# A fused retention and SwiGLU kernel: the first segment in another order, weight words and side tables in fewer transfers

## The chip, the cores and the metric

The kernel runs on one core of a Trainium2 chip. The metric is the device time of one execution in microseconds (us). A core has five engines that run side by side, each through its own list of instructions in order: TensorE (PE; loads of its stationary operand are shown as PEld), VectorE (DVE), ScalarE (ACT), GpSimd (POOL) and SyncE (SP), which here issues nearly all transfers (DMA). Matrix products land in PSUM, here eight banks of 128 x 512 floats; everything else lies in SBUF.

## The reference

Retention with a decay per head, then a gated feed-forward block, in 32-bit floats:

```python
B, H, S, D = 4, 8, 768, 64            # q, k, v
gamma = 1.0 - 2.0 ** (-5.0 - np.arange(H))
for t in range(S):
    state = gamma * state + einsum('bhd,bhe->bhde', k[:, :, t], v[:, :, t])
    y[:, :, t] = einsum('bhd,bhde->bhe', q[:, :, t], state) / sqrt(D)
x = y.transpose(0, 2, 1, 3).reshape(3072, 512)
g = x @ w_gate                        # 512 x 1536
out = (g * sigmoid(g) * (x @ w_val)) @ w_out   # 1536 x 512
```

The weights come in as 64-bit floats and are read as pairs of 32-bit words.

## The kernel before

**Tiling.** Retention is computed in chunks of 128 positions. For a chunk, the scores `k q` are masked with a decay table; y is the old state times the scaled q plus own values times the masked scores; the state is carried on with a scaled k. The 3072 tokens are cut into four segments of 768 (3 chunks of each of two sequences). Each segment goes through three stages: retention makes xT; the up stage walks over 12 units of 128 of the 1536 features; the down stage adds up 6 x 12 products in six banks. Each 2 x 2 block product of the up stage is done with seven products instead of four (Strassen's scheme in Winograd's form), of sums of x and of differences of weights. In segments 1 to 3 operands are split in three parts for a faster product form (L826, L876); in segment 0 products are in plain 32-bit floats (L665). The retention of the next segment runs as side steps within a down stage (L903 to L960).

**Segment 0.** Six chunks are loaded (`cs`, in order: pairs of first, second and third positions of two sequences). While its up stage runs, the weights are brought in: 24 pieces, 0 to 11 up (128 features of w_gate and w_val, 1 MB of words) and 12 to 23 down (w_out, 0.5 MB). A piece is loaded (L170), converted from two words to one float in five steps, turned into differences (L251) or split (L236), and stored to DRAM for the later segments. The conversion: `a` on ACT rescales the high word (L209), `b` on ACT makes the sign bits in a PSUM bank (L213), `S` on DVE joins them (L223), `c` on ACT scales the low word (L217), `C` on POOL adds it (L232). The raw words lie in the buffers `rawp` and `loads`; a load waits on SP until the piece before it in its buffer is through with `C`.

**The order is written out by hand** in strings of tokens. A token is a letter, a number and perhaps a part: `l4:1` loads q (0 is k transposed, 1 q transposed, 2 v, 3 k) of chunk 4; `A` loads a piece of the decay tables; `s` scores, `m` values and the copy of y to xT (L483), `x` sums of x (L635), `t` state, `g` decay of a state, `k`/`q` scaling on POOL, `K`/`Q` on DVE, `w` warm-up products; `U` loads a weight piece into a buffer, `a b S c C` convert it, `T` makes differences, `F` splits, `Z` stores; `L` loads a side table (L498), `P` loads inputs of segment 1; `M` multiplies gate and value of a unit (L679). `START` (L291) runs before the up stage. `beside` (L297) is a list of 73 slots parted by `|`, six for each of the 12 units: `up` (L655) runs a slot after each of its parts through `aside` (L389). Since every engine keeps its order, a token's place fixes its place in the list of each engine that it uses.

**A unit of the up stage** (L683 to L703), in PE's order: B11 times x11 into bank x, copied to `p1` by ACT (L684); the gates product of the unit before, which waits for that unit's DVE add L698, since it goes on in the bank that L698 reads; T1 times s1 into wb, copied to `p5` (L689); T2 times s2 into x, copied to `u2` (L692); B22 times s4 into wb, which goes on after the copy L689, and the add L695; T3 times s3 into x, and the add L698; B21 times x12 into z, and the add L701. A product is four matmul records of 384 columns here.

**Side steps.** Two chunks are worked at once, one of each sequence. `scale_k2` (L599) scales k of a chunk by eight activations on ACT, one a head. `load_side` (L498) brings in the masks of one group of heads for one half of the partitions: a full part, and a shifted part that keeps the second 64 positions. Planned times in `WHEN` (L325) order the side steps. `finish` (L880) takes a finished bank to SBUF, on DVE for odd tiles and on ACT for even ones, and stores it.

Of the kernel before, what the change touches and what calls it, by code (L numbers as in the profile page):

```python
# [17 lines left out]
P = 128  # L18
# [7 lines left out]
L = 3  # L26
# [23 lines left out]
def tile_retnet_swiglu(  # L50
# [101 lines left out]
    T3, B22, B12, T1, B11, B21, T2, T4 = 0, 1, 2, 2, 3, 4, 5, 6  # L152
# [17 lines left out]
    def load_piece(piece, where=0):  # L170
        kind, a = piece
        wide = w_gate.dtype != F32
        if kind == "up":
            new_wt(a)
            gate, val = (w[:, ts(a, P)].rearrange("(c p) f -> p c f", p=P)
                         for w in (w_gate, w_val))
            parts = [(val[:, ds(KH, KH)], 0), (val[:, ds(0, KH)], 1), (gate, 2)]
        else:
            parts = [(w_out[ts(a, P)], 0)]
# [4 lines left out]
        for src, i in parts:  # L184
            if wide:
                src = src.bitcast(U32)
            t = to[:, i:].rearrange("p a b -> p (a b)")
            if kind == "up":
                c = src.shape[1]
                t = t[:, : c * src.shape[2]].rearrange("p (c f) -> p c f", c=c)  # L190
            nc.sync.dma_start(out=t, in_=src)  # L191

    signs = {}
    stores = {}

    def words_of(piece):
        w, slot, n = span(piece)
        d = w[:, ds(slot, n)].rearrange("p a b -> p (a b)")
        r = raw[piece].rearrange("p a (n two) -> p (a n) two", two=2)
        return d, r[:, :, 0], r[:, :, 1]  # L200


    def convert_a(piece, own, part=None):


        if piece in raw:
            d, lo, hi = words_of(piece)
            if part in (0, None):
                act(d, hi.bitcast(F32), AF.Copy, scale=2.0 ** -112)  # L209
            if part in (1, None):  # L210
                signs[piece] = []
                for i, o in enumerate(own):
                    act(banks[o].bitcast(I32), d[:, ts(i, 512)], AF.Prelu, scale=2.0 ** 94,  # L213
                        alpha=2.0 ** 127)
                    signs[piece].append(banks[o])
            if part in (2, None):
                act(lo.bitcast(I32), lo, AF.Copy, scale=2.0 ** -29)  # L217

    def convert_b(piece):
        if piece in raw:  # L220
            u = words_of(piece)[0].bitcast(U32)
            for i, t in enumerate(signs.pop(piece)):
                stt(u[:, ts(i, 512)], u[:, ts(i, 512)], 3, t.bitcast(U32),  # L223
                    op0=ALU.logical_shift_left, op1=ALU.bitwise_or)


    def convert_c(piece, halves=1):
        if piece in raw:
            d, lo, hi = words_of(piece)
            n = d.shape[1] // halves  # L230
            for i in reversed(range(halves)):
                pool(d[:, ts(i, n)].bitcast(I32), d[:, ts(i, n)].bitcast(I32),  # L232
                     lo[:, ts(i, n)].bitcast(I32), op=add)
            del raw[piece]
# [16 lines left out]
    def sums_t(piece, parts=range(3)):  # L251
# [5 lines left out]
        for o, x, y in [((pair, w[:, ds(B22, 2)], w[:, ds(B12, 2)])),  # L257
# [3 lines left out]
        if parts[-1] == 2:  # L261
# [5 lines left out]
    sign_banks = {0: (0, 1), 1: (4, 5)}  # L267

    parts = {
        "s": lambda n: scores(cs[n]), "m": lambda n: mix(cs[n]), "x": lambda n, *p: sums_x(n, *p),  # L270
        "g": lambda n: decay(cs[n]), "t": lambda n: state(cs[n]), "w": lambda n: warm_up(n),
        "k": lambda n: scale_k(cs[n]), "q": lambda n: scale_q(cs[n]),
        "K": lambda n: scale_k(cs[n], nc.vector), "Q": lambda n: scale_q(cs[n], nc.vector),
        "S": lambda n: convert_b(pieces[n]),
        "C": lambda n: convert_c(pieces[n], 1 + (n == 0)), "T": lambda n, *p: sums_t(pieces[n], *p),
        "U": lambda n, p: load_piece(pieces[n], p[0]), "l": lambda n, p: load_chunk(n, p[0]),
# [3 lines left out]
        "L": lambda n: load_side(n // 2, n % 2),  # L280
        **{p: lambda n, i=i: convert_a(pieces[n], sign_banks.get(n, (6, 7)), i)
           for i, p in enumerate("abc")}}

    def do(order):
        for o in order.split():
# [6 lines left out]
        l0:0 l1:0 A0 A1 l0:2 l1:2 A2 l0:3 l2:0 l2:1 l1:3 l2:2 l2:3 l3:0 l3:1 l3:2 l3:3 l4:0  # L292
        l4:1 U0:0 l4:2 l5:0 l5:1 l5:2 U1:2 l4:3 l5:3 s0 w6 s1 m0 m1 K0 t0 K1 s2 t1 g2 g3 Q2
        s3 m2 x0:0 x0:1 x0:2 x0:3 k2 q3 t2 s4 a0 b0 m3 k3 t3 q4 c0 s5 S0 x1:0 x1:1 x1:2 x1:3
        m4 a1 q5 C0 U2:0 m5 x2:0 T0:0 x2:1 T0:1 x2:2 x2:3 T0:2 U3:4 U12:6
    """
    beside = """  # L297
        b1 | c1 S1 U13:7 | g5 g4 C1 | a2 T1:0 U14:8 | U15:9 | c2 b2 T1:1 a3 |
        S2 T1:2 | b3 C2 Z0 S3 | Z1 T2:0 | c12 c3 a12 C3 M0 b12 | U5:0 a13 T2:1 | T2:2 |
        S12 C12 T3:0 M1 |  | T3:1 F12:0 U4:2 Z2 | T3:2 a4 b4 U6:4 S4 a5 Z3 | F12:1 c4 F12:2  # L300
            C4 | b5 S5 T4:0 |
        T4:1 c6 L0 | M2 U16:6 c5 C5 | b13 c13 S13 | L1 C13 U7:2 a6 a14 | F12:3 T5:0 U8:0 b6
            | T4:2 T5:1 S6 F13:0 |
        F13:1 Z4 F13:2 b14 | F13:3 Z13 C6 M3 S14 | a15 a7 b7 c7 | T5:2 T6:0 T6:1 Z12 | S7
            T6:2 Z5 L3 c14 b15 | C14 U18:8 F14:0 |
        S15 C7 F14:1 | M4 F14:2 F14:3 | a8 U9:4 U17:7 Z6 c15 | C15 a16 Z14 | L2 F15:0 T7:0 |
            F15:1 c8 b8 |
        T7:1 S8 | U10:2 F15:2 a9 M5 C8 F15:3 | a17 T7:2 c16 b16 | U19:9 T8:0 b9 | U11:0 S16
            P0 C16 S9 F16:0 | P1 b17 |
        F16:1 T8:1 F16:2 Z15 c9 | T8:2 F16:3 Z7 | a10 Z16 S17 c10 C9 | c17 M6 C17 | U22:4  # L310
            a19 U20:6 F17:0 T9:0 a18 F17:1 | T9:1 b10 |
        k4 Z8 U21:7 b18 | S10 C10 a11 F17:2 S18 | M7 U23:5 c18 F17:3 | T10:0 T9:2 | b19 Z9
            b11 C18 F18:0 | T10:1 F18:1 F18:2 S11 P2 c19 Z17 c11 |
        T10:2 S19 F18:3 M8 a20 | b20 C11 | c20 S20 | a21 b21 T11:0 | a22 S21 C19 C20 | T11:1
            T11:2 t4 c21 Z18 F19:0 |
        F19:1 F19:2 k5 F20:0 Z10 F19:3 | b22 F20:1 t5 C21 a23 b23 | F21:0 S22 c22 M9 F21:1
            Z11 F20:2 | c23 F20:3 C22 Z19 | S23 F22:0 C23 F21:2 | F21:3 Z20 |
        F23:0 F22:1 Z21 F22:2 | M10 F22:3 Z22 | F23:1 F23:2 |  | F23:3 | |
        Z23
    """.split("|")  # L320
    sign_banks = {0: (0, 1), 1: (4, 5), 3: (4, 6), 12: (7,), 19: (4,), 20: (7,), 21: (6,), 22: (7,), 23: (6,), 4: (6, 7), 5: (6, 7), 6: (6, 7), 7: (6, 7), 8: (6, 7), 9: (6, 7), 10: (6, 7), 11: (6, 7), 13: (4,), 14: (4,), 15: (4,), 16: (4,), 17: (4,), 18: (4,), 2: (6, 7)}
# [92 lines left out]
    def scores(c):  # L414
        kt, qt = (pairs(chunks[c][w]) for w in range(2))
        sp = [bank("s") for i in range(2)]
# [6 lines left out]
        for i in range(2):  # L423
            j = turn["a"] = turn.get("a", -1) + 1
            t = pairs(tmp[:, ts(j % 4, 512)])
# [5 lines left out]
    def scale_q(c, engine=nc.gpsimd):  # L431
        if c % NCK:
            qt = pairs(chunks[c][1])
            engine.tensor_tensor(qt, qt, qdec, op=ALU.mult)

    def scale_k(c, engine=nc.gpsimd):
        if c % NCK < NCK - 1:
            kd = chunks[c][3].rearrange("p (h d) -> p h d", h=H)
            engine.tensor_tensor(
                kd, kd, kdec[:, :, None].to_broadcast([P, H, D]), op=ALU.mult)  # L440
# [26 lines left out]
    def mix(c):  # L467

        ci, seq, pos = c % NCK, c // NCK % 2, ts(c % L, P)
        qd, vn = pairs(chunks[c][1]), chunks[c][2]  # L470
        a = att.pop(c)
        prev = state_of(c, 1)
        y = pairs(banks[(0, 1, 2, 3, 7, 6)[first_chunks.index(c)]])
        own = [(n, i, y[ds(D * i, D), n]) for n in range(NP) for i in range(2)]
        for k, (n, i, to) in enumerate(own if ci else []):
            r = ds(D * i, D)
            nc.tensor.matmul(to, prev[r, n], qd[r, n], start=k < 2, stop=False,
                             skip_group_check=True)
        for k, (n, i, to) in enumerate(own):
# [576 lines left out]
```

## Time and profile before

| | us |
|---|---|
| median of 3 runs | 675.24 (674.68 to 676.48) |
| profiled execution, its own time | 675.8 |
| its span, first to last instruction | 674.0 |
| span up to the first up product | 28.93 |
| up stage of segment 0, to the last of its products | 28.93 to 148.35 |
| three later segments and the rest | 148.35 to 674.0 |

The groups of the up stage of segment 0 in the page's table of groups (line, engine, operation, output and inputs, count; then busy time and mean ns; then the idle time before them and what ended it):

```profile
L665 PE MATMUL bank<-first 128*128 128x384 f32 x336 | 112.4, 494 | 5.3 <-DVE hT L698 4.8
...
L232 POOL TENSOR_TENSOR first<-first,rawp 128x1024 int32<-128x1024 int32 (+1 forms) x21 | 41.3, 1973 | 38.0 <-DVE first L223 14.7
```

A mean of PE records is above the time from one to the next, since records overlap. The five 5 us stretches that begin the up stage, by engine (length; busy time and count of PE, PEld, DVE, ACT, POOL; clock; share of the DMA engines; GB/s):

```profile
25.00:30.00 5.00, 5.00 (x67) 3.92 (x66) 4.23 (x9) 2.80 (x4) 3.75 (x3) 1.00 0.37 129
30.00:35.00 5.00, 4.63 (x15) 2.56 (x14) 3.64 (x9) 4.05 (x10) 1.02 (x2) 1.00 0.66 202
35.00:40.00 5.00, 5.00 (x17) 2.88 (x17) 2.98 (x6) 4.35 (x10) 1.44 (x1) 1.00 1.06 387
40.00:45.00 5.00, 4.87 (x16) 2.55 (x15) 2.99 (x6) 5.00 (x11) 2.51 (x1) 1.00 1.02 383
45.00:50.00 5.00, 5.00 (x17) 2.97 (x16) 5.00 (x10) 3.34 (x6) 2.40 (x1) 1.00 1.03 398
```

Each row counts an engine as busy when it carries out an instruction, so PE reads full also where its clock is granted at half; the clock column tells the two apart.

### The profile page before, as it was taken

How to read it: one execution, taken by the hardware profiler on the slowest of the kernel's cores; microseconds unless marked ns; L12 is line 12 of the kernel's file. 1: busy time of each engine (PE TensorE's matmuls, PEld its weight loads, DVE VectorE, ACT ScalarE, POOL GpSimd, SP SyncE). 2: the span in 40 equal slices, each digit the busy share in tenths (PEclk: the TensorE clock that was granted, in tenths of full speed). 3: DMA queues.
4: the chain of work that ended last, by engine and by line, in shares of the span. 5: the costliest groups of instructions: out<-in, count | busy, mean ns of one | idle time of the engine just before them, and what ended most of it. 6: DMA issues, size and time to landing. Idle time of an engine off the chain costs nothing.

```text
span 674.0 us, 12402 instructions
## 1 busy us (share of the span) xinstructions
PE 658.8 (98%) x4724; PEld 550.1 (82%) x4724; DVE 465.5 (69%) x742; ACT 387.3 (57%) x793; POOL 250.2 (37%) x164
## 2 busy tenths in 40 slices
PE   8898899999999999999998999999999999999997
PEld 7654455567778999997776999998777899999886
DVE  3765988986787766675777676666776876667541
ACT  3586779756637555545648656555474755554221
POOL 1443557640103665550100566562010655653000
PEclk9998999999999999999998999999999999999999
DMA  9798999966675533466774443364767444313553
GB/s 334 252 379 293 327 317 403 402 226 212 216 256 220 193 111 110 159 201 200 239 234 181 146 168 110 109 213 157 237 225 223 183 180 143 131 65 133 187 187 140
DMA packets 49723, 141.59 MB, mean 210 GB/s; under 512 B 6144, under 2 KB 18944, under 8 KB 49664
## 3 DMA queue, kind: packets, MB, share of 16 engines
q1 hardware_dynamic: 49376, 140.28, 59.6%
q8 instruction: 37, 0.61, 0.4%
q10 hardware_dynamic: 288, 0.52, 0.2%
q14 instruction: 22, 0.18, 0.1%
HBM read 114.04 MB, written 26.74 MB: 209 GB/s over the span
## 4 chain that ended last, share of the span: by engine, by line
PE 87%; DMA 6%; DVE 3%; ACT 1%; issue 1%; SPq 1%; POOL 0%; ACTq 0%; DVEq 0%; POOLq 0%
PE bank L826 39%; PE bank L876 30%; PE bank L665 11%; PE bank L522 6%; DMA rawp<-in_w_gate_dram 2%; DMA rawp<-in_q_t_dram 1%; DMA hT<-in_k_n_dram 1%; DMA hT<-in_k_t_dram 1%; DMA hT<-in_q_t_dram 1%; SPq L191 1%; DVE first L80 1%; DVE first L223 0%; DVE oitem L739 0%; POOL first L232 0%; ACT chunk_x L761 0%
## 5 line engine op out<-in xcount | busy, mean ns | idle before, releaser
L826 PE MATMUL bank<-x,gitem 128*128 128x384 f32 x1296 | 231.7, 335 | 0.0
L826 PEld LDWEIGHTS bank<-x,gitem 128*128 128x128 f32 x1296 | 226.0, 188 | 0.7 <-ACT tmp L841 0.2
L876 PE MATMUL bank<-oitem,gitem 128*128 128x512 f32 x864 | 216.4, 403 | 0.2 <-DVE hT L844 0.2
L876 PEld LDWEIGHTS bank<-oitem,gitem 128*128 128x128 f32 x864 | 159.8, 189 | 41.4 <-issue 2.9
L726 POOL TENSOR_TENSOR gitem<-gitem 128x768 fp32r<-128x768 f32 x72 | 138.5, 1943 | 120.8 <-DVE gitem L723 112.7
L665 PE MATMUL bank<-first 128*128 128x384 f32 x336 | 112.4, 494 | 5.3 <-DVE hT L698 4.8
L665 PEld LDWEIGHTS bank<-first 128*128 128x128 f32 x336 | 63.7, 192 | 52.2 <-DVE hT L698 6.1
L720 ACT ACTIVATE gitem<-loads 128x768 fp32r<-128x768 f32 x72 | 58.2, 841 | 35.9 <-issue 29.4
L595 POOL TENSOR_TENSOR loads<-loads,tab 128x512 f32<-128x512 f32 x8 | 12.7, 1585 | 142.8 <-PE bank L522 142.8
L723 DVE SCALAR_TENSOR_TENSOR gitem<-gitem,loads 128x768 fp32r<-128x768 f32 x72 | 65.5, 951 | 0.0
L720 ACT ACTIVATE gitem<-hT 128x768 fp32r<-128x768 f32 x48 | 40.1, 839 | 36.7 <-PE bank L876 24.5
L723 DVE SCALAR_TENSOR_TENSOR gitem<-gitem,hT 128x768 fp32r<-128x768 f32 x48 | 45.8, 960 | 18.3 <-ACT gitem L720 18.3
L232 POOL TENSOR_TENSOR first<-first,rawp 128x1024 int32<-128x1024 int32 (+1 forms) x21 | 41.3, 1973 | 38.0 <-DVE first L223 14.7
L80 DVE SCALAR_TENSOR_TENSOR gitem<-gitem 128x768 fp32r<-128x768 f32 x48 | 46.0, 964 | 0.8
L761 ACT COPY chunk_x<-bank 64x256 f32<-64x256 f32 x72 | 25.6, 368 | 34.6 <-PE bank L522 33.9
L826 PE MATMUL bank<-x,oitem 128*128 128x384 f32 x216 | 43.8, 338 | 0.0
L842 ACT COPY tmp<-bank 128x384 f32<-128x384 f32 x36 | 17.2, 479 | 46.0 <-PE bank L826 44.3
L726 POOL TENSOR_TENSOR oitem<-oitem 128x256 fp32r<-128x256 f32 x36 | 28.5, 793 | 29.5 <-DVE oitem L723 28.2
L843 DVE TENSOR_TENSOR hT<-bank,tmp 128x384 f32<-128x384 f32 x36 | 20.1, 557 | 27.0 <-PE bank L826 27.0
L845 DVE TENSOR_TENSOR hT<-hT,bank 128x384 f32<-128x384 f32 x36 | 19.9, 553 | 26.9 <-ACT bank L845 26.9
L826 PEld LDWEIGHTS bank<-x,oitem 128*128 128x128 f32 x216 | 38.1, 188 | 0.0
L841 DVE TENSOR_TENSOR tmp<-bank,tmp 128x384 f32<-128x384 f32 x36 | 20.0, 557 | 20.2 <-PE bank L826 20.2
(93 smaller groups left out, 725.2 us busy)
## 6 DMA issues: line engine op xcount, KB each, us to landing
oitem<-wdnt SPq DMA_DIRECT2D x45, 768.0 KB, 4.4
loads<-wup SPq DMA_DIRECT2D x36, 896.0 KB, 4.7
wup<-first SPq DMA_DIRECT2D x12, 896.0 KB, 8.6
wdnt<-oitem SPq DMA_DIRECT2D x12, 768.0 KB, 5.0
rawp<-in_w_val_dram SPq DMA_DIRECT2D x24, 256.0 KB, 6.2
rawp<-in_w_gate_dram SPq DMA_DIRECT2D x12, 512.0 KB, 6.9
out_dram<-chunk_x SPq DMA_DIRECT2D x24, 256.0 KB, 2.2
loads<-in_k_t_dram SPq DMA_DIRECT2D x18, 256.0 KB, 3.4
```

What stands on the lines that cost most here:

```text
L80: stt(o, x, 1.0, y, op0=mul, op1=op)
L232: pool(d[:, ts(i, n)].bitcast(I32), d[:, ts(i, n)].bitcast(I32), lo[:, ts(i, n)].bitcast(I32), op=add)
L522: nc.tensor.matmul(o, a, b, start=start, stop=True, skip_group_check=True)
L665: nc.tensor.matmul(o, w[:, slot, k], a[:, k], start=(start and k == 0), stop=(stop and k == KH - 1), skip_group_check=True)
L720: act(o[0], x, AF.Copy, scale=CUT / FAR)
L723: stt(o[1], f32(o[0]), -FAR, x, op0=mul, op1=add)
L726: op(o[2], f32(o[0]), f32(o[1]), op=add)
L761: copy(cx[half[i], ds(2 * h, 2), c], y_both(h, i, c))
L826: nc.tensor.matmul(o, w[:, a, k], xs_of[s][:, a, OP[p], k], start=start and a == k == 0, stop=a == 2 and k == KH - 1, skip_group_check=True)
L841: steps = (lambda: copy(p1, x), lambda: tt(c11, z, p1, op=add), lambda: act(gate, c11, AF.Silu, scale=ONE), lambda: copy(u2, x), lambda: c ...
L843: lambda: copy(p5, wb), lambda: tt(h1, x, p5, op=add),
L876: nc.tensor.matmul(banks[tok], hs[f][:, a, ds(i * TH + u * P, P)], wo[f][:, a], start=f == a == 0, stop=f == NF - 1 and a == 2, skip_group ...
```

## The change

- `START` and `beside` are written anew: other places for nearly all tokens. The warm-up products `w6` go. In `START`, k of chunks 2 to 5, q of 4 and 5 and v of 5 move about; piece 0's gate words are loaded before its value words (`U0:0`, then `V0:0`).
- The scaled q goes to a buffer of its own in `loads` instead of over q, so that it needn't wait for the scores. `mix` is cut in two: the products with the old state (`o`, `mix_old`) and those with own values (`m`). Scores of chunks 1 and 3 use another pair of banks.
- Piece 0 is converted in two halves, gate and value words (`a0:1`, `a0:0` and so on).
- The first two products of unit 0 that need no sums, B11 and B21, come before its slots (`p0`, `p1`, the new `begin`).
- Up pieces are loaded in two transfers instead of three, with their row blocks in reverse order; slots B11 and B21 change places, and each product takes x in reverse order as well.
- `load_side` issues one transfer instead of four; the shifted part is copied from the full one by ACT (`h`, `high_side`).
- k of the third pair's first chunk is scaled on POOL in one instruction.
- The very last output tile leaves in two halves, on ACT and DVE, and by the ACT and the SP queue.

A token `r` (`rows_of`, k turned by a product instead of loaded) is defined, but neither order uses it.

```diff
-    T3, B22, B12, T1, B11, B21, T2, T4 = 0, 1, 2, 2, 3, 4, 5, 6
+    T3, B22, B12, T1, B21, B11, T2, T4 = 0, 1, 2, 2, 3, 4, 5, 6
...
-            parts = [(val[:, ds(KH, KH)], 0), (val[:, ds(0, KH)], 1), (gate, 2)]
+            parts = [(val, 0), (gate, 2)]
...
-        for src, i in parts:
+        for src, i in parts[take]:
...
+                src = src[:, ::-1]
             nc.sync.dma_start(out=t, in_=src)
...
+    def part_of(own, half):
+
+        if half is None:
+            return own, slice(None)
+        return own[half : half + 1], ts(half, 512)
...
-        for o, x, y in [((pair, w[:, ds(B22, 2)], w[:, ds(B12, 2)])),
+        for o, x, y in [((pair, w[:, ds(B22, 2)], w[:, B12 : B11 + 1 : 2])),
...
     START = """
-        l0:0 l1:0 A0 A1 l0:2 l1:2 A2 l0:3 l2:0 l2:1 l1:3 l2:2 l2:3 l3:0 l3:1 l3:2 l3:3 l4:0
-        l4:1 U0:0 l4:2 l5:0 l5:1 l5:2 U1:2 l4:3 l5:3 s0 w6 s1 m0 m1 K0 t0 K1 s2 t1 g2 g3 Q2
-        s3 m2 x0:0 x0:1 x0:2 x0:3 k2 q3 t2 s4 a0 b0 m3 k3 t3 q4 c0 s5 S0 x1:0 x1:1 x1:2 x1:3
-        m4 a1 q5 C0 U2:0 m5 x2:0 T0:0 x2:1 T0:1 x2:2 x2:3 T0:2 U3:4 U12:6
+        l0:0 l0:2 l1:0 A0 A1 A2 l1:2 l0:3 l2:1 l2:0 l1:3 s0 l2:2 l3:0 l3:1 l5:2 l3:3 l2:3
+        U0:0 l3:2 l4:0 l4:1 l5:0 l5:1 s1 V0:0 l4:2 m0 m1 K0 K1 t0 s2 l4:3 g2 t1 Q2 s3 o2
+        l5:3 q3 o3 m2 a0:1 k2 k3 x0:0 U1:2 t2 x0:1 x0:2 m3 x0:3 g3 t3 s4 b0:1 x1:0 q4 c0:1
+        x1:1 S0:1 o4 s5 a0:0 b0:0 x1:2 c0:0 q5 o5 m4 C0:1 m5 S0:0 C0:0 x1:3 x2:0 T0:0 a1 p0
+        T0:1 x2:1 b1 p1 U2:0 x2:2 U14:8
     """
     beside = """
-        b1 | c1 S1 U13:7 | g5 g4 C1 | a2 T1:0 U14:8 | U15:9 | c2 b2 T1:1 a3 |
-        S2 T1:2 | b3 C2 Z0 S3 | Z1 T2:0 | c12 c3 a12 C3 M0 b12 | U5:0 a13 T2:1 | T2:2 |
-        S12 C12 T3:0 M1 |  | T3:1 F12:0 U4:2 Z2 | T3:2 a4 b4 U6:4 S4 a5 Z3 | F12:1 c4 F12:2
-            C4 | b5 S5 T4:0 |
...
+        c1 S1 T0:2 | x2:3 g5 C1 |  | U3:4 U13:7 T1:0 | c2 g4 a2 T1:1 U15:9 | b2 U12:6 |
+        Z0 T1:2 | S2 a3 C2 T2:0 M0 T2:1 | Z1 a12 | b3 c3 U5:0 b12 | S3 T2:2 a13 | C3 c12 |
+         | a5 U4:2 S12 T3:0 L0 | C12 M1 L1 | F12:0 U6:4 T3:1 a4 | T3:2 F12:1 b4 S4 c4 | C4
+            b5 S5 c6 T4:0 |
...
-        sp = [bank("s") for i in range(2)]
+        sp = [bank("y" if cs.index(c) % 2 and cs.index(c) < 4 else "s") for i in range(2)]
...
             qt = pairs(chunks[c][1])
-            engine.tensor_tensor(qt, qt, qdec, op=ALU.mult)
+            chunks[c][1] = loads[:, ts(cs.index(c) + 2, 512)]
+            engine.tensor_tensor(pairs(chunks[c][1]), qt, qdec, op=ALU.mult)
...
-        for i in range(2):
-            nc.sync.dma_start(out=side[g][half[m], i, : 2 * P], in_=cols[half[0], i])
-            nc.sync.dma_start(
-                out=side[g][half[m], i, 2 * P :].rearrange("p (n t) -> p n t", n=2),
-                in_=cols[half[1], i].rearrange("p (n t) -> p n t", n=2)[:, :, D:])
+        nc.sync.dma_start(out=side[g][half[m], :, : 2 * P], in_=cols[half[0]])
...
+    def high_side(g):
+
+        low, high = (side[g][:, :, c].rearrange("p i (n t) -> p i n t", n=2)
+                     for c in (ds(0, 2 * P), ds(2 * P, P)))
+        for i in range(2):
+            copy(high[:, i], low[:, i, :, :D])
...
         dec = kdec_b if i else kdec
+        if p == 2 and i == 0:
+            pool(kd, kd, dec[:, :, None].to_broadcast([P, H, D]), op=mul)
+            return
...
-                nc.tensor.matmul(o, w[:, slot, k], a[:, k], start=(start and k == 0),
+                nc.tensor.matmul(o, w[:, slot, k], a[:, KH - 1 - k], start=(start and k == 0),
...
+        def begin(n):
+            if n == 0:
+                product(x, B11, a_up(0, 0))
+                nc.scalar.copy(p1, x)
+            else:
+                product(z, B21, a_up(0, 1))
+                tt(c11, z, p1, op=add)
...
+        if s == NSEG - 1 and tok == 5:
+            a, b = (ds(n * DM // 2, DM // 2) for n in range(2))
+            act(t[:, a], banks[tok][:, a], AF.Copy, scale=scale)
+            nc.scalar.dma_start(out=out[ds(row, P), a], in_=t[:, a])
+            nc.vector.tensor_scalar(t[:, b], banks[tok][:, b], scale, None, op0=mul)
+            nc.sync.dma_start(out=out[ds(row, P), b], in_=t[:, b])
+            return
```

## The prediction

> **What bounds the kernel now.** I read the page first, then PE's waits, then the granted clock in one-microsecond stretches around each wait, then the other engines' timelines there.
>
> The page's row of engines, and the row of clocks in 40 slices of 16.85 us:
>
> ```profile
> PE 658.8 (98%) x4724; PEld 550.1 (82%) x4724; DVE 465.5 (69%) x742; ACT 387.3 (57%) x793; POOL 250.2 (37%) x164
> ...
> PEclk9998999999999999999998999999999999999999
> ```
>
> TensorE is busy 98% of the span, so only three things are to be had: the opening, in which PE does small products at the pace of arriving inputs; PE's waits; and the slices with clock 8. These are PE's waits over the whole span (total, times, longest):
>
> ```profile
> PE bank L665 <- DVE hT L698: 4.8, 2, 2.7
> PE bank L522 <- ACT chunk_x L761: 2.2, 1, 2.2
> PE bank L420 <- DMA rawp<-in_q_t_dram: 1.4, 1, 1.4
> PE bank L420 <- DMA hT<-in_q_t_dram: 1.1, 1, 1.1
> ```
>
> The first row is two waits in the up phase of the first segment, at 57.36 and 80.0. The second is one wait at 360.09. Rows three and four belong to the opening. The stretches after two of them (columns: stretch, length, busy PE, PEld, DVE, ACT, POOL, then clock, DMA share, GB/s):
>
> ```profile
> 60.00:61.00 1.00, 0.96 (x2) 0.66 (x3) 1.00 (x2) 1.00 (x2) 0.14 (x1) 0.50 1.02 302
> 61.00:62.00 1.00, 1.00 (x3) 0.52 (x2) 0.75 (x3) 1.00 (x3) 1.00 (x1) 0.50 0.88 168
> 62.00:63.00 1.00, 1.00 (x3) 0.58 (x2) 0.58 (x1) 0.20 (x1) 1.00 (x1) 0.50 0.98 387
> ...
> 364.00:365.00 1.00, 1.00 (x4) 0.78 (x3) 1.00 (x3) 1.00 (x3) 0.00 (x0) 0.50 0.81 115
> 365.00:366.00 1.00, 1.00 (x4) 0.81 (x3) 1.00 (x3) 1.00 (x4) 0.00 (x0) 0.50 0.73 294
> 366.00:367.00 1.00, 1.00 (x3) 0.73 (x3) 1.00 (x2) 1.00 (x4) 0.00 (x0) 0.50 1.04 437
> ```
>
> PE counts as busy there and does half the work. Each drop lasts about 3.3 us, so it costs some 1.65 us on top of its wait.
>
> **The opening: -2.0 us.** PE starts its first up product (L683) at 28.93. From 15.09, when chunk 3's q lands (wait of 1.1), it has one more wait, 1.37 for the last q at 23.75, so its own work from there is 28.93 - 15.09 - 1.37 = 12.5. The new order of loads places chunk 3's q 16th instead of 17th in 256 KB units, and moves two units of w_val and one v of the last pair behind the last q, which becomes 26th instead of 28th. The landings 15.05 and 23.61 lie 11 units apart, 0.78 a unit (four of them of weights); plain units take about 0.69. So chunk 3's q lands near 14.4 and the last q near 22.1. The products of old states (L477) now stand ahead of those of own values and need only q: PE can run without a gap from 14.4, 14.4 + 12.5 = 26.9. POOL carries the scalings (1.28 each, L434) beside it: the last q at 22.1 to 23.4, then the gate half of piece 0 (1.27), done at 24.7, before 26.9. Scaling into another buffer also frees POOL from waiting for the score products. The last pair's first v is unit 29, about 24.5; it is wanted at 25.0. Bounds: -2.8 if the overlap is better, +0.5 if v or scaling comes late.
>
> The six warm-up products go (L293, w6: 1.60 us, all of it in idle PE time). PE then has holes of about 1.6 us near 6 to 8 and 1 near 9. The records granted 1.00 through similar holes at 14 and 22.4, so I cost it at nothing; if the clock fell there, slack up to 14.4 hides most of it, with up to 2 us if the half clock reaches past 14.4.
>
> **The up phase: -5.4 us.** It runs from 28.93 to 148.35 = 119.4. Its 336 records cost 44.52/136 = 0.327 each undisturbed (chain piece at 82.16), 110.0; with two state products (0.61 and 0.62) and a first down product (0.70) inside, 111.9. So 7.5 is lost: waits 5.3 and slow clock.
>
> Why the wait at 57.36: DVE works in order, and the adds of unit 2 that PE waits for (L698) stand behind the sign step of piece 4 (L223), whose weights landed at 56.28. Piece 4's load stands on SP behind piece 5's, which waited until 43.5 for POOL to finish piece 2 (L232, 40.96 to 43.47). DMA was idle 63% and 34% of the time in 25-30 and 30-35, because SP waited for piece 0's conversion until 30.10. After the change:
>
> - Both first products that need no sums (B11, B21: 8 records, 2.6 us) lie at 26.9 to 29.5 and cover the last sums, piece 0's value half (weights about 23.8; ACT 1.9, DVE 0.64, POOL 1.27 to 27.2) and its differences (0.69). The old 0.37 wait at 30.86 goes. Piece 2's load can be issued at 27.2 instead of 30.1.
> - Piece 1 lands near 28.5 (unit 35, against 33). Its steps (ACT 1.15 + 1.12 + 1.15) stand on ACT ahead of the copies L684 and L689, and PE's fourth product waits for L689: ACT reaches it near 32.4, done 32.9, against PE's wish at 32.15. A new wait of 0.7; bounds 0 and 2.
> - Pieces 2, 14, 3, 13, 15, 12 and two stores come to 6.1 MB; at 0.385 MB/us from 28.5 that ends near 44, piece 5 near 47 to 49, piece 4 near 50 to 51, six earlier than 56.28. Besides, piece 4's sign step moves from unit 2's fourth slot, ahead of L698, to its fifth, behind it. What it holds now is L701 and so the gates of unit 2, wanted near 57.5. I cost this wait at zero.
> - Piece 5's first step (a5) moves on ACT from unit 2's fourth slot to its second, ahead of the copy L692. ACT's list puts piece 2's sign bits near 38.7 and POOL's end of piece 2 near 42.7, so piece 5 is issued hardly earlier than before (43.5). Unit 1 begins near 29.5 + 4 x 1.31 + 0.7 = 35.4, unit 2 near 44.6, its T3, which needs L692, near 51.1. Landing 48.5 plus 1.16 and 0.48 is 50.1. I take 0.4, bounds 0 and 3.7 (at the old landing, 44.71 + 6.9 = 51.6, 2.1 of wait and a clock drop).
> - The second wait (at 80) is DVE overloaded from 68.9 to 82: three subtractions that take 0.41 alone took 2.43 together while POOL ran its piece (79.84 to 81.34), and one L739 took 2.52 against 0.43. The Trainium skill says why (SBUF — State Buffer, "Who interferes with whom"): a DVE operation with two SBUF inputs and a GpSimd operation that reads SBUF exclude each other. DVE's work isn't less after the change, only earlier and spread otherwise; I leave 1.0 of 2.16.
>
> Sum of what remains: 0.7 + 0.4 + 1.0 = 2.1 of 7.5, a gain of 5.4; bounds -1 (a loss: all as before and a wait more) and 7.
>
> **Fewer transfers: nothing by itself.** Up pieces go in two transfers instead of three (12 issues less of about 0.42), side tables in four instead of sixteen (12 less of about 0.6). SP isn't the bound: no PE wait ends on it. The 1.1 MB of loads per piece is the same. The shifted halves come from four ACT copies (about 0.3 each, between 0.25 for 64 columns at L446 and 0.37 for 256 at L761), in stretches where ACT is busy 23 of 30 us; 1.2 of cover is there. If it is not, 0.3 at most each time.
>
> **The boundary at 360: -3.5 us.** ACT's timeline (start, length):
>
> ```profile
> 353.62 2.03 ACT L603 ACTIVATE loads<-loads,tab 128x64 f32<-128x64 f32 x8 [7.81 <-DMA loads<-in_k_n_dram]
> 355.56 0.83 ACT L720 ACTIVATE gitem<-hT 128x768 fp32r<-128x768 f32 x1
> 356.29 1.04 ACT L741 ACTIVATE x<-x 128x1024 fp32r<-128x1024 f32 x1
> 357.24 2.01 ACT L603 ACTIVATE loads<-loads,tab 128x64 f32<-128x64 f32 x8
> 359.27 2.92 ACT L761 COPY chunk_x<-bank 64x256 f32<-64x256 f32 x8
> ```
>
> The second L603 group is the one sent to POOL (third pair, first chunk; no other boundary has it, since the third pair of the others has no next state). The copies L761 were ready when PE finished at 357.09, so they begin 1.92 earlier and PE waits 0.24 instead of 2.16. POOL is empty after 350.2; its 1.04 (L439, same operation) to 1.59 (L595) lie near 353.6, six microseconds ahead of need. Two rules speak against it. GpSimd's exclusion of DVE would hold L723 at 354.12 by up to 1.6; DVE has 3.47 of idle before 361.83, so the sum stays. And the clock: the Trainium skill (TensorE: Matmul & The Clock Gate, "HAM oscillation") warns of PE gaps above about 3.4 us; by it a gap of 2.16 costs no clock, and the gain is 1.9. The trace has half clock after the gaps of 2.16 and of 2.68, though not after the 2.16 at 80. The row decides: 1.9 + 1.6 = 3.5. Bounds 1.5 and 3.6.
>
> **The end: -0.4 us.** The last tile goes out in halves, ACT and DVE side by side: 0.69 (L887) becomes about 0.42 (a 128x256 DVE row), and two transfers of half size on two queues replace one of 2.0. Bounds -0.7 and +0.3.
>
> **Sum.** 2.0 + 5.4 + 3.5 + 0.4 = 11.3: span 674.0 to 662.7, own time 675.8 to 664.5. The profiled execution lies 0.56 above the median shown, 675.24, so I predict 663.9.
>
> **Rivals.** (1) *The up phase gains nothing net* (20%): a late piece on ACT with its clock drop (3.7), the wait near 32 and the DVE overload replace the old waits. For it: piece 5's step moves forward in ACT's order while POOL's end of piece 2 hardly moves. Against: the DMA gap of 25-35 closes. 663.9 + 5.4 = 669.3. (2) *The clock falls in the opening* (10%), since w6 is gone: 663.9 + 2 = 665.9. Against: holes like these are at 1.00 now. (3) *The boundary keeps its clock drop*, or another place gets one (10%): 663.9 + 1.6 = 665.5. (4) *Slower* (5%): ACT's in-order list holds PE for a late weight piece again and again. Without any wait in the up phase the time would be 675.24 - 2.0 - 7.5 - 3.5 - 0.4 = 661.8; each piece that comes 3.3 behind its slot costs 5.0 with its drop. From three such pieces on it is slower: 676.8. Against: after 82 no piece was late, and the last up load was issued at 99.7 while PE needed until 148.
>
> The forecast has 55%, its own range 661 to 667. With the rivals I give 660.5 to 670.5, leaving out (4) and the worst of (1). A measurement of this kernel can tell 0.3% (2.0 us) from no change; below 673.2 is faster: all of the forecast, (2), (3) and nearly all of (1), 93%; 2% same, 5% slower.
>
> **What would show it.** First L665 near 27; no wait on L698 near 57 and the clock row free of 8s; a short PE wait on ACT near 32, perhaps one near 51; state product at 360 without a wait; last transfers of 128 KB. A clock below 1 in the first 20 us, or PE waits over 4 us in the up phase, would make it wrong.

## The result and the profile after

| | before | changed |
|---|---|---|
| median, us | 674.96 (4 runs, 673.8 to 676.48) | 668.54 (4 runs, 667.77 to 669.52) |
| ratio, with its 95% interval | | 0.9904 (0.988 to 0.9929) |
| span of the profiled execution, us | 674.0 | 667.7 |

The change gains 6.4 us where 11.3 were forecast. The time lies inside the stated range of 660.5 to 670.5, but outside the forecast's own range of 661 to 667. The row of clocks on the changed kernel's page:

```profile
PEclk9999999999999999999999999999999999999999
```

Both slices with clock 8 are gone. PE's two longest waits in the changed kernel (total, times, longest). Line numbers have moved: L716, L729 and L732 are the ACT copies that were L684, L689 and L692; L738 is the add that was L698.

```profile
PE bank L695 <- ACT tmp L716: 1.4, 1, 1.4
PE bank L695 <- ACT tmp L732: 1.1, 1, 1.1
```

Where the 6.3 us between the two spans lie, stage by stage, by the same products in both profiles:

| stage | before | changed | difference | forecast |
|---|---|---|---|---|
| to the first up product | 28.93 | 29.08 | +0.15 | -2.0 |
| up stage of segment 0 | 119.42 | 115.20 | -4.22 | -5.4 |
| from there to segment 2's up stage | 227.29 | 224.16 | -3.13 | -3.5 |
| from there to the end | 298.36 | 299.26 | +0.90 | -0.4 |

**Opening.** PE's timeline of the changed kernel, around the end of the opening (start, length, then the idle time before it and what ended it):

```profile
21.25 0.54 PE L506 MATMUL bank<-tmp,hT 128*64 128x128 f32 x5 [1.07 <-issue]
...
24.48 1.75 PE L428 MATMUL bank<-rawp 64*128 64x128 f32 x16
...
29.08 23.49 PE L695 MATMUL bank<-first 128*128 128x384 f32 x72
```

The last scores take 1.75 instead of 1.16: they wait for DVE to read the previous chunk's scores out of the same two banks. The hole of 1.07 differs from execution to execution. With this opening, the profiles of seven kernels below have the first up product at 27.70 to 28.86 (27.87, 27.70, 27.93, 28.07, 27.74, 27.81 and 28.86), and where the waits of these name a releaser for L506 besides DVE, it is the landing of a v, with 0.2 to 0.8. The opening before the change has it at 28.79 to 28.93 in four profiles (before, runs 2, 6 and 10; in run 11, where a q came late, at 30.81). So the opening gains about 1.0 typically; this profile is a late one.

**Up stage.** ACT's timeline of the changed kernel near both waits:

```profile
52.16 1.13 ACT L218 ACTIVATE first<-rawp 128x1024 f32<-128x1024 f32 x1 [1.65 <-DMA rawp<-in_w_gate_dram]
53.19 0.47 ACT L732 COPY tmp<-bank 128x384 f32<-128x384 f32 x1
...
56.01 1.14 ACT L218 ACTIVATE first<-rawp 128x1024 f32<-128x1024 f32 x1 [1.83 <-issue]
...
60.31 1.12 ACT L224 ACTIVATE rawp<-rawp 128x1024 int32<-128x1024 uint32 x1
61.32 0.46 ACT L716 COPY tmp<-bank 128x384 f32<-128x384 f32 x1
```

The first row is a5, which holds L732 as the prediction said it might. The third is a4: piece 4 is usable at 56.0, about as late as before (56.28, a4 at 56.40), not at 50 to 51; with the earlier openings of runs 3, 4 and 8 it is usable at 54.7 to 55.0. Its steps b4 and c4, and b5 and c6 (the fourth row), then stand ahead of L716, and PE waits for that. So the weights are hardly earlier; what the order changed is how far PE gets before it misses them. Instead of one wait of 2.68 at 57.36, behind which the clock fell, there are 1.14 at 52.6 and 1.41 at 60.4, and the clock held. (The last section shows why two shorter waits keep it.)

The reason for the late weights shows in the DMA share. The changed kernel in stretches of 2 us (columns as above; the last two are DMA share and GB/s):

```profile
28.00:30.00 2.00, 2.00 (x25) 1.56 (x22) 1.02 (x3) 1.36 (x3) 1.28 (x1) 1.00 0.03 9
...
52.00:54.00 2.00, 0.86 (x3) 0.29 (x2) 0.78 (x3) 1.84 (x3) 0.00 (x0) 1.00 1.14 275
54.00:56.00 2.00, 2.00 (x7) 1.14 (x7) 1.27 (x4) 0.18 (x1) 1.44 (x1) 1.00 1.12 257
```

The gap in the loads is still there, up to 31.5: piece 2's load was issued at 29.97 (28.60 to 28.77 in runs 3, 4 and 8), not at 27.2, since POOL finished piece 0 at 29.94. POOL waited for DVE, whose list was full: the last masks at 26.33 to 27.53, a sum, and the second half's sign step only at 27.86. In 52 to 56 the DMA engines show as busy as elsewhere but move some 265 GB/s, where 350 to 430 are usual from 32 to 52; side tables and piece 6 are under way there. In run 12, where the side tables come later, the same two stretches have 347 and 419.

**DVE.** The groups of one DVE step between 25 and 150 us, the last of a split (count, then busy time and mean ns), first before, then after the change:

```profile
L739 DVE TENSOR_SCALAR oitem<-oitem 128x512 fp32r<-128x512 f32 x12 | 13.4, 1117 | 0.1
```

```profile
L779 DVE TENSOR_SCALAR oitem<-oitem 128x512 fp32r<-128x512 f32 x12 | 9.3, 780 | 0.1
```

The same twelve steps cost 4.1 us less. That fits fewer meetings with POOL's operations, but no run tests it, and the rule that the prediction cites speaks of DVE operations with two SBUF inputs, while this step reads one. With it the wait of 2.16 at 80 has gone; one of 0.17 is left, at 114.

**Boundary into segment 2.** ACT's copies now follow at once on the step before them (L781, to 353.55), and PE's state product comes at their end. ACT:

```profile
353.56 2.93 ACT L801 COPY chunk_x<-bank 64x256 f32<-64x256 f32 x8
```

PE:

```profile
356.58 1.15 PE L551 MATMUL bank<-loads 128*64 128x64 f32 x32 [0.64 <-issue]
```

PE's wait is 0.64 (the row names no releaser; ACT's last copy ends at 356.49), and the granted clock stays at 1.00. POOL's scaling took 1.04, from 347.78.

**End.** The tail after PE's last product is 4.12 instead of 3.71. The chain of waits, its last steps:

```profile
663.97 0.39 ACT chunk_x L928
...
664.39 0.42 DVE chunk_x L930
```

The halves run one after the other: ACT's half waits for the store of tile 1, which used the same buffer and landed at 663.86, and DVE's half starts after ACT's.

### The profile page after: what moved, and what is told of

It reads as the page before. It is cut to its first block, busy times and chain, and to the rows that moved or that the text cites. A ratio compares the mean times of both kernels' runs of the same rounds, so it can differ in the third digit from the quotient of the medians.

```text
span 667.7 us, 12348 instructions
## 1 busy us (share of the span) xinstructions
PE 655.4 (98%) x4712; PEld 547.5 (82%) x4712; DVE 463.1 (69%) x742; ACT 386.2 (58%) x792; POOL 252.0 (38%) x165
## 4 chain that ended last, share of the span: by engine, by line
PE 82%; DMA 8%; DVE 3%; ACT 2%; issue 2%; SPq 1%; POOL 1%; ACTq 0%; POOLq 0%; DVEq 0%
PE bank L866 39%; PE bank L916 29%; PE bank L695 6%; PE bank L551 6%; DMA rawp<-in_w_gate_dram 2%; DMA loads<-in_w_out_dram 1%; DMA oitem<-wdnt 1%; DMA tab<-in_decays_dram 1%; DMA wdnt<-oitem 1%; SPq L194 1%; DMA hT<-in_q_t_dram 1%; POOL first L237 1%; ACT bank L221 1%; DVE first L231 0%; ACT chunk_x L801 0%
## 5 line engine op out<-in xcount | busy, mean ns | idle before, releaser
L695 PE MATMUL bank<-first 128*128 128x384 f32 x336 | 110.8, 489 | 2.8 <-ACT tmp L716 1.4
L885 DVE TENSOR_TENSOR hT<-hT,bank 128x384 f32<-128x384 f32 x36 | 19.9, 553 | 27.2 <-ACT bank L885 27.2
```

Source lines behind the costliest of these rows:

```text
L695: nc.tensor.matmul(o, w[:, slot, k], a[:, KH - 1 - k], start=(start and k == 0), stop=(stop and k == KH - 1), skip_group_check=True)
```

## The experiments

Each ran beside the kernel before on the same chip, whose medians were 675.09, 674.84 and 675.13 in the three groups (runs 1 to 4, 5 to 8, 9 to 12). The changed kernel's 668.54 is that of the table above. Two theories stand behind the choice. Mine: the gain is the boundary's wait with its clock drop, and the rest is a better fit of late weights to PE, which the order alone makes. The rival: fewer transfers bring the weights sooner, and the boundary gives only its wait.

**1. The boundary undone in the changed kernel.**

```diff
-        if p == 2 and i == 0:
-            pool(kd, kd, dec[:, :, None].to_broadcast([P, H, D]), op=mul)
-            return
```

> The changed kernel with the third pair's scaling of k back on ACT, all else as changed. Theory A (wait and clock): PE waits about 2.2 us again at the boundary into segment 2 and the granted clock falls to a half for about 3.3 us after it, so the time is 3.0 to 3.5 us above the changed kernel's 668.5, near 671.7. Theory B (the wait alone counts, as the rule of 3.4 us would have it): about 1.5 us above, near 670.0, with the clock at 1.00.

671.48 us (16 runs), 2.9 above the changed kernel; ratio to before 0.9951 (0.9937 to 0.9965). One of its stretches at half clock, 359 to 362, behind a PE wait of 1.83 (the clock is the third figure from the end):

```profile
360.00:361.00 1.00, 1.00 (x4) 0.78 (x3) 1.00 (x4) 1.00 (x3) 0.00 (x0) 0.50 0.68 222
```

Theory A: half clock after a wait shorter than the old one. This execution also ran at half clock from 7.44 to 10.85, after a wait of 1.79 for k in the opening, where the dropped products `w6` used to stand.

**2. The boundary alone, in the kernel before.** The same three lines, added.

> The kernel before with only the third pair's k scaled on POOL. Theory A: it gains what the boundary gained in the changed kernel, 3.1 us of 675, ratio near 0.9954, with PE's wait near 360 down to 0.2 to 0.7 and no half clock after it. Theory B: the clock falls there anyway, the gain is 1.5 us, ratio near 0.9978.

672.12 us (14 runs), ratio 0.9958 (0.9945 to 0.9971): 3.0 gained. PE's wait at the boundary is 0.37 and the clock 1.00 behind it. Both directions give the same 3 us, so nearly half of the change's gain is this one instruction.

**3. The last tile in one piece.** `finish` as before the change.

```diff
-        if s == NSEG - 1 and tok == 5:
...
-            return
```

> The changed kernel with the last tile stored as before, in one piece by DVE and SP. From the end of PE's last product to the end of the span the kernel before took 3.71 us and the changed one 4.12. Theory A (the halves cost, since ACT's half waits for a buffer and DVE's half waits for ACT's): 3.7 again, 0.4 us faster than the changed kernel. Theory B (the halves gain and the difference was chance): 4.5, 0.4 us slower. The time alone can hardly tell 0.4 us, the span's end can.

668.45 us, ratio 0.9915 (0.9891 to 0.9939), no difference. From PE's end (661.57) to the end of the span (665.6) 4.0. DVE had waited 0.4 after PE's end for the store of tile 1, as ACT's half does. Neither theory: the halves neither cost nor gain.

**4. The halves in buffers of their own.**

```diff
-            act(t[:, a], banks[tok][:, a], AF.Copy, scale=scale)
...
-            nc.vector.tensor_scalar(t[:, b], banks[tok][:, b], scale, None, op0=mul)
...
+            ta, tb = kept_vk[:, 0, : DM // 2], tab[:, : DM // 2]
+            act(ta, banks[tok][:, a], AF.Copy, scale=scale)
...
+            nc.vector.tensor_scalar(tb, banks[tok][:, b], scale, None, op0=mul)
```

> The changed kernel with the two halves of the last tile in two SBUF areas of their own. Theory A (the reuse of the second tile's buffer and the shared tile make the halves wait): both halves start within 0.2 us of PE's end, and the tail falls from 4.12 to about 3.3 us, 0.8 us faster than the changed kernel. Theory B (DVE and ACT can't read one PSUM bank side by side): DVE's half still starts after ACT's, tail about 3.8.

668.04 us, ratio 0.9897 (0.9881 to 0.9913). DVE's half in the kernel's timeline:

```profile
662.57 0.42 DVE L931 TENSOR_SCALAR tab<-bank 128x256 f32<-128x256 f32 x1 [1.13 <-ACT kept_vk L929]
```

ACT's half now begins at 662.15, when PE ends (662.12), so the buffer was its wait; DVE's still follows ACT's, though only the PSUM bank is shared. The tail stays at 4.2: theory B in its mechanism, with no gain at all. Whether the chip or the program's own ordering makes DVE wait was not tried.

**5. The two late steps moved behind the copies that they hold.**

```diff
-         | a5 U4:2 S12 T3:0 L0 | C12 M1 L1 | F12:0 U6:4 T3:1 a4 | T3:2 F12:1 b4 S4 c4 | C4
-            b5 S5 c6 T4:0 |
-        F12:2 | Z2 T4:1 c5 | L3 T4:2 c13 C5 M2 | b13 U16:6 a6 S13 | T5:0 a14 C13 T5:1 h0 b6
+         | U4:2 S12 T3:0 L0 | a5 C12 M1 L1 | F12:0 U6:4 T3:1 a4 | T3:2 F12:1 b4 S4 c4 | C4
+            b5 S5 T4:0 |
+        c6 F12:2 | Z2 T4:1 c5 | L3 T4:2 c13 C5 M2 | b13 U16:6 a6 S13 | T5:0 a14 C13 T5:1 h0 b6
```

> The changed kernel with two tokens moved: a5 one slot later (behind the copy of unit 2 that PE waits for near 52.6) and c6 one slot later (behind the copy of unit 3 that PE waits for near 60.4). Theory A (these steps of late pieces hold ACT's copies): the wait near 52.6 (0.9 to 1.2) goes, the one near 60.4 (1.3 to 1.7) shrinks by c6's 1.1 us, the time falls by 1.5 to 2.2 us, to near 666.5. Theory B (the pieces' landing itself is what PE is short of, and the wait only moves to a later instruction): the same sum of waits, no gain.

669.0 us, ratio 0.9922 (0.9901 to 0.9943). Its PE waits:

```profile
PE bank L695 <- ACT tmp L716: 2.5, 1, 2.5
```

Theory B: the wait at 52.6 goes and adds itself to the one at 60, 2.47 where there were 1.14 + 1.41, and here the clock fell after it. It is piece 4's landing that PE is short of.

**6. The step that held PE at 57.36, moved in the kernel before.**

```diff
-        S12 C12 T3:0 M1 |  | T3:1 F12:0 U4:2 Z2 | T3:2 a4 b4 U6:4 S4 a5 Z3 | F12:1 c4 F12:2
+        S12 C12 T3:0 M1 |  | T3:1 F12:0 U4:2 Z2 | T3:2 a4 b4 U6:4 a5 Z3 | S4 F12:1 c4 F12:2
```

> The kernel before with one token moved: the sign step of piece 4 on DVE one slot later, behind the add L698 of unit 2. Theory A (this one place made the wait at 57.36 with its clock drop): the wait of 2.7 goes and the clock stays at 1.00 near 60; ACT's steps of pieces 4 and 5 are late still and may hold the copy of unit 3, so 2 to 4 us faster than before, near 672. Theory B (piece 4 is late for everything behind it): less than 1 us, the wait appears on an ACT copy with the same length.

674.97 us (14 runs), ratio 0.9999 (0.9983 to 1.0016): nothing. The wait on L698 at 57 is gone in its profile and stands on ACT's copies instead, 1.07 and 0.66. Theory B, as in the run before: with weights as late as these, moving this one token gained nothing.

**7. All transfers as before, in the changed order.**

```diff
-            parts = [(val, 0), (gate, 2)]
+            parts = [(val[:, ds(KH, KH)], 0), (val[:, ds(0, KH)], 1), (gate, 2)]
...
-        nc.sync.dma_start(out=side[g][half[m], :, : 2 * P], in_=cols[half[0]])
+        for i in range(2):
+            nc.sync.dma_start(out=side[g][half[m], i, : 2 * P], in_=cols[half[0], i])
+            nc.sync.dma_start(
+                out=side[g][half[m], i, 2 * P :].rearrange("p (n t) -> p n t", n=2),
+                in_=cols[half[1], i].rearrange("p (n t) -> p n t", n=2)[:, :, D:])
```

(and the tokens `h0` and `h1` taken out)

> The changed kernel with the transfers as before: up pieces in three, side tables in sixteen with their shifted halves from DRAM, without ACT's four copies. Theory A (fewer transfers bring nothing by themselves): within 0.7 us of the changed kernel, ratio to before near 0.990. Theory B (SP's issues delay the weights behind them): pieces 4 to 8 land 1 us or more later, the waits near 52.6 and 60.4 grow, 2 us or more slower than the changed kernel.

674.3 us (14 runs), ratio 1.0001 (0.999 to 1.0013). My theory A fell: without fewer transfers nothing of the gain is left. The boundary's part is still there in its profile (PE's wait is 0.5, the clock 1.00); it is outweighed by a wait of 5.71 that ends at 66.1, with half clock from 65.07 to 71.89.

**8. B21 of unit 0 in its old place.**

```diff
-        if f:
-            begin(1)
+        begin(1)
```

(and `p1` taken out of `START`)

> The changed kernel with the product B21 of unit 0 back in its old place, after T3, so that only B11 covers the last sums and piece 0's differences. Theory A (the early product covers 0.5 to 0.9 us of waiting, and gives ACT time before the copy L729): PE waits 0.5 to 0.9 us for the differences near 30 and the time grows by 0.5 to 1 us. Theory B (ACT's copies are the bound there): the wait only moves from the copy L729 to the differences, no change beyond 0.3 us.

668.28 us, ratio 0.9911 (0.9894 to 0.9928). No change, as theory B had it, but not by its way: PE waits 0.28 for the differences near 29.6, and the wait near 52 is 0.60, where it is 1.14 in the changed kernel and 0.88 and 1.20 in runs 3 and 4. What is lost at the start is waited less for the late weights. (Waits of 0.6 to 0.7 on the copy L729 stand in the profiles of runs 3 and 4, but at 127 us.) The early second product brings nothing.

**9. Only the side tables as before.** The second half of the edit of run 7.

> The changed kernel with only the side tables as before, in sixteen transfers without ACT's copies; up pieces stay in two. With all old transfers the kernel lost its whole gain (674.3). Theory A (the ten issues of side tables that now stand ahead of piece 6's load on SP delay it by about 6 us, and ACT's step c6 holds PE): nearly all of that loss is here too, a PE wait of 4 to 6 us near 61 with a half clock after it, 673 to 674.5. Theory B (the pieces' three transfers are the cost): within 1 us of 668.5.

673.41 us (17 runs), ratio 0.9974 (0.996 to 0.9988): 4.9 of run 7's 5.8 above the changed kernel. SP's timeline of this run; L527, L528 and L532 are side tables, L194 is piece 6:

```profile
46.01 2.01 SPq L527 DMA_DIRECT2D tab<-in_decays_dram  x1
...
56.24 0.53 SPq L194 DMA_DIRECT2D rawp<-in_w_val_dram  x1
```

SP's waits between 44 and 57 us (total, times, longest):

```profile
SPq L528 <- DMA rawp<-in_w_val_dram: 1.3, 1, 1.3
SPq L527 <- DMA rawp<-in_w_gate_dram: 1.1, 1, 1.1
```

ACT's timeline of it:

```profile
62.69 1.10 ACT L224 ACTIVATE rawp<-rawp 128x1024 int32<-128x1024 uint32 x1 [3.88 <-DMA rawp<-in_w_gate_dram]
```

Ten issues hold SP from 46.0 to 56.1: 7.3 us go to the issues themselves and 2.4 to two waits for the landing of piece 4's words, at 52.61 and 54.34. In all the traces of this case, wherever an issue on SP waits for a landing, it is that of the transfer eight issues before it; here the seventh and the eighth side table wait for the two transfers of piece 4. So here the number of transfers counts more than their size: the DMA engines' share falls to 0.64 in 52 to 54 and 0.24 in 54 to 56 while piece 6 stands behind. It is asked for at 56.24. In the changed kernel four issues take from 46.98 to 51.2, and it is asked for at 51.30. Here c6 waits for piece 6, the copy L720 (L716 of the changed kernel) waits behind c6, PE waits 5.05 for the copy, and then runs for over 5 us at half clock. Theory A.

**10. The new transfers in the old order.** Reordered slots, two transfers a piece, `load_side` in one and `high_side` added to the kernel before.

```diff
-        S15 C7 F14:1 | M4 F14:2 F14:3 | a8 U9:4 U17:7 Z6 c15 | C15 a16 Z14 | L2 F15:0 T7:0 |
+        S15 C7 F14:1 h0 | M4 F14:2 F14:3 | a8 U9:4 U17:7 Z6 c15 | C15 a16 Z14 | L2 F15:0 T7:0 |
...
-        T7:1 S8 | U10:2 F15:2 a9 M5 C8 F15:3 | a17 T7:2 c16 b16 | U19:9 T8:0 b9 | U11:0 S16
+        T7:1 S8 | U10:2 F15:2 a9 M5 C8 F15:3 | a17 T7:2 c16 b16 | U19:9 T8:0 b9 | U11:0 S16 h1
```

> The kernel before, in its own order, with the new transfers: up pieces in two, side tables in four and ACT's copies. Theory A (fewer transfers are worth something only in the new order, where side tables stand ahead of weights): within 1 us of before, ratio 0.9985 to 1.0015. Theory B (they save SP time everywhere): 2 us or more faster, ratio below 0.997.

675.06 us (22 runs), ratio 0.9985 (0.997 to 1.0001). Theory A: 0.1 by the medians and 1.0 by the ratio, whose interval reaches from nothing to 2.0; in the new order they are worth 5.8.

**11. One heavy DVE step moved, in the kernel before.**

```diff
-        F13:1 Z4 F13:2 b14 | F13:3 Z13 C6 M3 S14 | a15 a7 b7 c7 | T5:2 T6:0 T6:1 Z12 | S7
-            T6:2 Z5 L3 c14 b15 | C14 U18:8 F14:0 |
+        F13:1 Z4 F13:2 b14 | C6 M3 S14 | a15 a7 b7 c7 | T5:2 T6:0 T6:1 Z12 | S7
+            T6:2 Z5 L3 c14 b15 | F13:3 Z13 C14 U18:8 F14:0 |
```

> The kernel before with one DVE step moved: the last step of the split of piece 13, which took 2.52 us at 74.77 because POOL was working, goes five slots later, with the store of that piece. Theory A (DVE overload made the wait at 80): the wait of 2.16 on L698 falls by 1.5 or more, the time by 1.5 to 2 us. Theory B (the wait follows from pieces that are late on POOL and ACT): DVE's list only idles where the step was, less than 0.5 us.

674.21 us (22 runs), ratio 0.9984 (0.997 to 0.9998), 0.9 us. PE runs there from 65.05 to 93.8 without a wait. Its timeline later:

```profile
114.72 11.88 PE L665 MATMUL bank<-first 128*128 128x384 f32 x36 [1.72 <-ACT tmp L692]
```

Between both: with the step gone the wait of 2.16 at 80 is gone too, though PE is there no later (about 79.4 by the records from 65.05 on, 80.0 before). So DVE's list did make it, but a new wait of 1.72 on ACT stands 33 us later. That it was POOL that made the step slow is not shown by this.

**12. Side tables behind the weights, late steps moved, a free bank for the last scores.** The edit of run 5, and

```diff
-         | a5 U4:2 S12 T3:0 L0 | C12 M1 L1 | F12:0 U6:4 T3:1 a4 | T3:2 F12:1 b4 S4 c4 | C4
+         | U4:2 S12 T3:0 | a5 C12 M1 | F12:0 U6:4 T3:1 a4 | T3:2 F12:1 b4 S4 c4 | C4
...
-        U7:2 a15 | a7 U8:0 | S14 c7 F12:3 c14 F13:3 Z12 Z4 C6 | b15 U9:4 M3 U17:7 | b7 T5:2
+        U7:2 a15 | a7 U8:0 L0 L1 | S14 c7 F12:3 c14 F13:3 Z12 Z4 C6 | b15 U9:4 M3 U17:7 | b7 T5:2
...
-        sp = [bank("y" if cs.index(c) % 2 and cs.index(c) < 4 else "s") for i in range(2)]
+        sp = [banks[0], banks[4]] if cs.index(c) == 5 else [
+            bank("y" if cs.index(c) % 2 and cs.index(c) < 4 else "s") for i in range(2)]
```

> The changed kernel with three moves: side tables L0 and L1 behind the load of piece 8 instead of ahead of that of piece 6 (and ACT's copies h0 later); a5 and c6 one slot later as in the run on those; the scores of the last chunk in a free pair of banks. Theory A (weights that land late are what is left of the up phase's loss, and side tables in their way are part of it): piece 4 lands near 54.5 instead of 56, the waits near 52 and 60 together fall from 2.5 to below 1, the opening gains 0.5, 665.5 to 667. Theory B (the lateness of piece 4 comes from the gap in the loads near 28 and stays): the waits stay at 2 or more, no faster than 668.

668.53 us, ratio 0.9894 (0.9874 to 0.9914), the same as the changed kernel. PE's timeline:

```profile
58.93 1.56 PE L696 MATMUL bank<-first 128*128 128x384 f32 x4 [1.08 <-ACT tmp L717]
61.14 41.89 PE L696 MATMUL bank<-first 128*128 128x384 f32 x128 [0.65 <-ACT tmp L730]
...
114.37 1.56 PE L696 MATMUL bank<-first 128*128 128x384 f32 x4 [1.69 <-DVE hT L739]
```

Neither theory. Each part helps a little: the opening ends at 27.31, 0.4 before the earliest seen without it; piece 4 is usable at 54.10; the waits near 52 and 60 fall from 2.55 to 1.73, not below 1. The 56.01 of the changed kernel's profile is no fair measure for piece 4, since that profile opens late; against runs 3, 4 and 8 with their 54.7 to 55.0 the move brings 0.6 to 0.9. And PE, now earlier, misses DVE's add at 113 by 1.69, so the time stays. None of the twelve is measurably faster than the changed kernel.

## Why the prediction was right in its direction and too large

The sum named the right places and was too large at each. That the time still lies in the stated range is owed to rival 1, whose 669.3 the range takes in, and not to the forecast.

- **Boundary, -3.5.** Right in mechanism, 3.0 by runs 1 and 2. The copies came 0.4 later against PE than the sum had them, so 0.64 of wait is left instead of 0.24. The row, not the rule, gave the clock's share. But here and in the up stage the sum took the two drops of one profiled execution as certain; of 110 executions of the kernel before, about a quarter have the mean clock that goes with two (last section).
- **Opening, -2.0.** Too large: about -1.0 typically and +0.15 in the profile that was compared. The term that failed is "PE can run without a gap from 14.4". The landing came at 14.98 (14.10 to 14.76 in the seven others), a v was late by up to 0.8, and a bank that two chunks share holds the last scores by 0.6, which the step did not look at. The fear for the clock without w6 (rival 2) was not empty: the clock stayed at 1.00 here and in six of the other seven profiles with this opening, and in run 1 it was half from 7.44 to 10.85, behind a wait of 1.79; the first up product came at 28.86 there, the latest of the seven. With w6 the opening can drop as well: in run 11, from 17.77 to 21.18, behind a wait of 2.82 for a late q.
- **Up stage, -5.4.** 4.2 by the profiles, made up otherwise than the step had it. Two of its terms failed. "Piece 2's load can be issued at 27.2" left out that the second half's sign step stands behind masks and sums in DVE's list; it was 29.97 (28.6 to 28.8 in earlier openings), the gap in the loads stayed, and piece 4 landed four to six later than worked out. And piece 4's place behind L698 did not make its wait zero: it came back through ACT, whose steps of pieces 4 to 6 stand ahead of the copy L716 (1.41). The a5 wait was 1.14, inside its bounds of 0 to 3.7 around 0.4; the 0.7 expected near 32 did not come; at 80 there is none, and 0.17 at 114, for the 1.0 that was left there. So 2.72 of waits remain instead of 2.1. The other 0.6 of the miss is a loss that the step counted as gone with the waits: waits of 5.21 and a drop of 1.70 make 6.9 of the 7.5, and the rest stayed. What was gained is 0.4 at 30.9, 2.0 of the wait at 80, 0.1 of the early waits, and the 1.7 of the clock drop after 57; together 4.2.
- **Fewer transfers, nothing.** The step that was plainly wrong. Its reason, that no PE wait ends on SP, was read from the old order. In the new one side tables stand ahead of piece 6 on SP, and sixteen transfers in place of four cost 4.9 us (run 9), all transfers 5.8 (run 7). In the old order no gain is clear of noise (run 10). So it was luck that the order could keep what it gained: it came together with the merged transfers that it needs.
- **End, -0.4.** +0.4 in the profile and no difference in runs 3 and 4: halves that follow one another gain nothing. Another 0.37 of the last stage's +0.9 is a wait for a weight transfer at 485.5, in a part that the change didn't touch.
- **Rivals.** The likeliest case had the order of size; the measured time lies near rival 1 (669.3), though by another way: the up stage did gain, and the opening, the tail and two terms of the up stage came out smaller.

## What to carry to other kernels

A transfer is priced by its place in the queue: ahead of a late load ten small ones cost 5 us, by the time of their issues and by waits for earlier landings, and behind the loads the same ten cost nothing clear of noise. When an engine list holds steps of late data, moving the step moves the wait; first ask when the data can land and what frees its buffer. And a short PE wait should be counted with the clock that may follow it.

## What the runs showed of the hardware that was not expected

**Which PE wait costs clock.** A wait of about 2 us was followed by half clock in some places and not in others. The traces tell which. In each of the 14 profiles the clock changes only at steps of 3.41 us, counted from its first record, and inside the work a half clock lasts one or two such windows. The windows lie elsewhere in each execution: that first record begins between 4.0 and 7.0 us. The kernel before, in its own windows behind two waits of 2.16 us (the busy time of PE is the second number, the clock the third from the end):

```profile
80.42:83.83 3.41, 1.68 (x5) 1.06 (x6) 3.41 (x6) 1.08 (x3) 1.33 (x2) 1.00 1.02 398
83.83:87.25 3.42, 3.42 (x12) 2.05 (x11) 1.96 (x5) 2.20 (x5) 3.28 (x2) 1.00 0.84 222
...
360.31:363.73 3.42, 1.49 (x34) 1.38 (x35) 1.79 (x4) 3.36 (x8) 0.00 (x0) 1.00 0.33 137
363.73:367.14 3.41, 3.41 (x10) 2.64 (x9) 3.41 (x7) 3.40 (x8) 0.00 (x0) 0.50 0.79 265
```

The wait at 80 is cut in two by the border at 80.42, and PE is still busy for 1.68 us in the second window; the clock stays. The wait at 360 falls almost whole into one window, PE is busy for 1.49, and the next window is at half. So it is in every window at full clock of these profiles, some 2700: behind the 26 with PE busy for up to 1.62 us (run 1, 4.03 to 7.44, has the most) the next one is at half, behind those with 1.68 or more it is not. It holds for two waits of 2.24 at 80 as well: in run 2 it falls into one window (1.18 busy) and half clock follows from 80.56 to 83.97; in run 6 a border cuts it (2.17 and 2.42 busy) and none follows. Where a window at half clock had PE busy for only 2.4 us, behind the waits of 5.05 (run 9) and 5.71 (run 7), the next was at half too. For a wait of this length it is therefore a matter of chance how it meets the windows; one that leaves PE busy for 1.7 us of each window was not followed by half clock here.

The Trainium skill (TensorE: Matmul & The Clock Gate, "What's actually happening") describes a window of about 3.4 us that runs freely and does not start with the kernel; the traces agree, with 3.41. Its advice to avoid gaps above 3.4 us (the same page, "HAM oscillation") is too mild for this kernel, by the 1.79 of run 1.

**The spread of the times.** It goes with these drops. One drop takes the mean clock of an execution of 674 us to 0.9975. Of the 110 executions of the kernel before that ran beside the experiments, the 13 with a mean clock of 0.999 or 1.00 took 672.4 us in the median, the 67 with 0.996 or 0.997 took 674.8, the 29 with 0.994 or 0.995 took 676.7, and one with 0.992 took 680.2. Of the changed kernel's four executions three are at 0.999 or 1.00, with a median of 668.2. By these medians an estimate: some 4.2 us of the gain remain between executions without a drop, and the other 2 are drops that come less often.
